# Weight loads issued from ScalarE's queue instead of SyncE's, with the list schedule's cost of such an issue changed

## The chip, the cores and the metric

The kernel runs on one core of a Trainium2 chip. The metric is device time in microseconds, the median of several executions. The engines are TensorE (PE; PEld is its weight load), VectorE (DVE), ScalarE (ACT), GpSimd (POOL) and SyncE (SP), which only issues DMA transfers. A q behind an engine's name (SPq, ACTq) is its instruction queue seen as an issuer of DMAs.

## What is computed

Three stages one after the other, on batch 4, sequence 576, model width 512 (8 heads of 64), in float32:

```
scores = scale * q @ k^T                      # 4 x 8 heads, 576 x 576
thresh = max(scores) - tau
scores = where(scores >= thresh, scores, -1e9)
attn   = softmax(scores) ;  x = attn @ v      # heads side by side: 4 x 576 x 512
h  = relu(x^T @ w_tok1) @ w_tok2              # mixes the tokens, 576 -> 256 -> 576
u  = x + h^T
x  = u + relu(u @ w_ch1) @ w_ch2              # 512 -> 1536 -> 512
h  = relu(x @ w_in)                           # 512 -> 1024
c  = 3-tap convolution of h along the sequence with conv_w
out = (h * sigmoid(c)) @ w_out                # 1024 -> 512
```

## The kernel before

**Arithmetic.** Most products run as three float16 passes over a high and a low half of each operand (`_h`, `_l`). Weights come from memory as float64 (two 32-bit words per element), are turned into float32 on the chip and split into halves. The scores of the first two batches are float32 matmuls.

**A piece of weights.** `load_hl` (L322) loads a piece of up to 128 x 512 elements (512 KB) into one of three buffers `st`. `wload` (L329) then turns it into float32 (`float32`, L355: ACT or POOL at L360/L362, ACT at L363, DVE at L364 and L366 into `wf`, of which there are two), makes the high half on ACT (L351) and the low half on POOL (L352). There are 47 such pieces, and the convolution's weights are one more small load through `load_hl`. A buffer `st` is free again when L363, L364 and L366 have read it, and only then may the load three pieces later start.

**Attention.** For each of 4 batches and 4 pairs of heads, `prep` (L441) loads `q`, `k` and `v` (`qt`, `kt`, `ld`); `scores` makes nine slots of 128 rows; `exps` takes the maximum on DVE (L548) and the exponential on ACT (L560), `mask` multiplies by the comparison on DVE (L567), `ph` and `rest` make two float16 halves (ACT L572, POOL L576), which a DMA transposes (L581; in the first batch inside `act_t`, later from `ph` to `pt`). `pv` multiplies by `v` (PE L591, L594), `norm` divides and splits into `xh` (ACT L619) and `xl` (POOL L620), `tok` does the token mixing.

**Dense part.** `dense(b)` holds both feed-forward layers of batch b (PE L758, L776, L809, L832). It runs beside the attention of batch b + 1. The first attention runs alone, with the first weight pieces beside it, up to about 106 us; the other pieces are turned beside `dense(0)`, up to about 280 us.

**Who orders the work.** All instructions are recorded first; then `Order.run` (L143) is a list scheduler: it keeps for each engine a time at which it is free, takes the earliest instruction by the program's order among those ready, adds a cost (`cost`, `send`), and fixes the order in which each engine issues. Each engine runs its own order strictly, so a waiting instruction holds all behind it. At most eight DMAs are under way in that order: eight semaphores (DMAHW0 to 7 below) serve all of them in turn. Before, SP issues every DMA except four small stores.

Of the kernel before, what the change touches and what calls it, by code (L numbers as in the profile page):

```python
# [11 lines left out]
I32 = mybir.dt.int32  # L12
# [8 lines left out]
class Order:  # L21
# [121 lines left out]
    def run(self):  # L143
        n = len(self.ins)
        left, ready, open_ = [len(b) for b in self.before], [0.0] * n, [False] * n
        later, now = {e: [] for e in self.LAG}, {e: [] for e in self.LAG}
        free, order = {e: 0.0 for e in self.LAG}, {e: [] for e in self.LAG}
        users, gone = {}, {}
        for u in self.uses:
            for t in u:  # L150
                users[t], gone[t] = users.get(t, 0) + 1, 0.0
        turn, slots, queue = {g: 0 for g in self.turns}, {g: [0.0] * self.bufs[g] for g in self.turns}, {g: [] for g in self.turns}
        end = start = queued = 0.0
        rows, tiled, lands = {}, False, []

        def offer(x):
            for t in self.first[x]:
                g = self.ring(t)
                if self.turns[g][turn[g]] != t or not slots[g]:
                    queue[g].append(x)  # L160
                    return
                ready[x] = max(ready[x], slots[g][0] + 40)
            open_[x] = True
            heapq.heappush(later[self.eng[x]], (ready[x], x))

        def again(g):
            held, queue[g] = queue[g], []
            for y in held:
                if not open_[y]:
                    offer(y)  # L170

        for x in range(n):
            if not left[x]:
                offer(x)
        for _ in range(n):
            t, e = min((free[e] if now[e] else max(free[e], later[e][0][0]), e) for e in free if now[e] or later[e])
            while later[e] and later[e][0][0] <= t:
                heapq.heappush(now[e], heapq.heappop(later[e])[1])
            x = heapq.heappop(now[e])
            if self.dma[x]:  # L180
                work, issue, least, land = self.send(x)
                if len(lands) >= 8:
                    t = max(t, lands[-8] + self.LAG["SP"])
                free[e] = t + 30 + issue
                if self.ins[x].opcode == "DmaTransposeAnt":
                    free[e] = max(free[e], queued)
                if e == "SP":
                    queued = max(queued, t + 700) + work
                    done = max(free[e] + least, queued + land)
                else:  # L190
                    done = max(free[e] + least, t + 700 + work + land)
                lands.append(done)
            elif e == "PE":
                work, (rt, ct), (r0, _) = self.cost(x), self.ins[x].tile_size, self.ins[x].tile_position
                wide = self.ins[x].ins[0].dtype == F32
                if rt < 128:
                    t = max(t, rows.get(r0, 0.0), start + 4, 0.0 if tiled else end + 95)
                    rows[r0], tiled = t + work, True
                    end, free[e] = max(end, t + work), t + 4
                else:  # L200
                    t = max(t, end + (95 if tiled else 0))
                    if ready[x] > end:
                        t = max(t, ready[x] + (250 if wide else 30))
                    rows, tiled, end, free[e] = {}, False, t + work, t + work
                start, done = t, t + work + 177
            else:
                work = self.cost(x)
                free[e], done = t + work - self.LAP[e], t + work + 12
            order[e].append(x)
            for z in self.first[x]:  # L210
                g = self.ring(z)
                turn[g] += 1
                heapq.heappop(slots[g])
                again(g)
            for z in self.uses[x]:
                users[z], gone[z] = users[z] - 1, max(gone[z], done)
                if not users[z]:
                    heapq.heappush(slots[self.ring(z)], gone[z])
                    again(self.ring(z))
            for z in self.after[x]:  # L220
                far = t + 1 if self.eng[z] == e == "PE" else done + self.LAG[self.eng[z]]
                ready[z] = max(ready[z], far)
                left[z] -= 1
                if not left[z]:
                    offer(z)
        for xs in order.values():
            for x, y in zip(xs, xs[1:]):
                self.tc.add_manual_dep(self.ins[y], self.ins[x].name, mybir.DependencyInfo(
                    mybir.DependencyClass.NoSync, mybir.DependencyReason.DATA), reason="order")
# [3 lines left out]
def kernel(ctx: ExitStack, tc: tile.TileContext, q, k, v, tau,  # L233
# [7 lines left out]
    nc = tc.nc  # L241
# [37 lines left out]
    V, A, G, T = nc.vector, nc.scalar, nc.gpsimd, nc.tensor  # L279
# [42 lines left out]
    def load_hl(src, o, n):  # L322

        st = stage.tile([P, 512, 2], I32, tag="st", name="st")
        nc.sync.dma_start(st[:, :n].rearrange("p n w -> p (n w)"), src.bitcast(I32)[:, 2 * o:2 * (o + n)])
        halves = st[:, :n].rearrange("p n w -> p (n w)").bitcast(U16).rearrange("p (n w) -> p n w", w=4)
        return halves[:, :, 1], st[:, :n, 1]

    def wload(src, dst, o, n, up, bank=None):  # L329

        hi, lo = [d[:, o:o + n] for d in dst]
        w = tmpp.tile([P, 512], F32, tag="wf", name="wf")[:, :n]
        if src.dtype == F32:
            nc.sync.dma_start(w, src[:, o:o + n])
            yield  # L340
            G.tensor_scalar(out=w, in0=w, scalar1=2.0 ** up, scalar2=1.0, op0=ALU.mult, op1=ALU.mult)
            whole = True
        else:
            lw, hw = load_hl(src, o, n)
            yield
            whole = up % 8 == 0
            f = ps[:, bank, :n] if bank is not None else w
            float32(w, f, lw, hw, up // 8, bank == CB)
        if not whole:
            G.tensor_scalar(out=w, in0=w, scalar1=2.0 ** up, scalar2=1.0, op0=ALU.mult, op1=ALU.mult)  # L350
        A.activation(out=hi, in_=w, func=AF.Copy)  # L351
        G.tensor_tensor(out=lo, in0=w, in1=hi, op=ALU.subtract)  # L352
        yield
# [51 lines left out]
    if conv_w.dtype == F32:  # L405
        nc.sync.dma_start(cw, conv_w)
    else:
        float32(cw, cw, *load_hl(conv_w, 0, 3 * NG), 0)
# [100 lines left out]
    free = [6]  # L509
# [363 lines left out]
    for b in range(B):  # L873
        att = attention(b + 1) if b + 1 < B else iter(())
        n = 0
# [66 lines left out]
```

## Time and profile before

| | before |
|---|---|
| median of 3 runs | 771.08 us (770.52 to 772.36) |
| the profiled execution | 773.05 us, span 771.2 us |
| PE busy | 721.5 us (94%) |
| DVE, ACT, POOL busy | 506.5, 459.0, 425.9 us |
| DMA share of the largest queue (SP's) | 58.2% |

The span runs from the first to the last instruction of the profiled execution; its own time has a little around it. In a timeline row stand start, duration, engine, line, operation, output<-inputs, and in brackets how long the engine stood idle before it and what ended that. The busy time of PE counts matmuls that overlap in the pipeline.

### The profile page before, as it was taken

Reading aid. Unit: us, or ns where it says so; the run is one execution under the profiler, and the core shown is the slowest. Engines: PE = TensorE matmul, PEld = TensorE weight load, DVE = VectorE, ACT = ScalarE, POOL = GpSimd, SP = SyncE. Lnnn points to the kernel's source line nnn. Section 1 sums busy time; section 2 is a strip of 40 time slices with the busy share of each in tenths; the row PEclk is TensorE's granted clock in tenths of the full one; section 3 lists DMA queues with packets and bytes.
Section 4 is the critical chain, followed back from the end, with each engine's and each line's share of the span. In section 5 each row is a group of like instructions: output and inputs, shape, how many; then the busy total and the mean of one; then the engine's idle time right before and its main releaser. Section 6 shows DMA issues by size and latency. Waiting matters only on the chain. (4 is left out here: it accounts for less than half of the span.)

```text
span 771.2 us, 18502 instructions
## 1 busy us (share of the span) xinstructions
PE 721.5 (94%) x7388; PEld 541.5 (70%) x7388; DVE 506.5 (66%) x913; ACT 459.0 (60%) x926; POOL 425.9 (55%) x463
## 2 busy tenths in 40 slices
PE   5779969999998789999999999999999999999998
PEld 3457757777776646788888766778888766878764
DVE  5968977887779971676867962676876951323470
ACT  6967857786758852576557753675656841211371
POOL 5967778887877990367464850367564830000040
PEclk9999989999999999999999999999999999999999
DMA  9999988999898602568876402577853400000001
GB/s 288 210 217 187 200 193 208 230 230 229 199 238 199 147 27 93 111 153 169 155 142 144 80 23 88 131 136 158 155 123 64 79 29 35 1 1 2 1 1 62
DMA packets 196199, 99.02 MB, mean 128 GB/s; under 512 B 174224, under 2 KB 177808, under 8 KB 196112
## 3 DMA queue, kind: packets, MB, share of 16 engines
q1 hardware_dynamic: 195792, 97.57, 58.2%
q8 instruction: 58, 0.95, 0.5%
q10 hardware_dynamic: 320, 0.26, 0.1%
q14 instruction: 29, 0.24, 0.1%
HBM read 43.54 MB, written 4.72 MB: 63 GB/s over the span
## 5 line engine op out<-in xcount | busy, mean ns | idle before, releaser
L576 POOL TENSOR_TENSOR ph<-e,ph 128x576 f16<-128x576 f32 x108 | 142.5, 1319 | 110.4 <-ACT ph L572 99.3
L776 PE MATMUL ps<-act_t,wc_h 128*128 128x256 f16 (+1 forms) x768 | 149.8, 286 | 0.0
L567 DVE SCALAR_TENSOR_TENSOR e<-ps,thr,e 128x576 f32<-128x576 f32 x108 | 87.9, 814 | 53.6 <-ACT e L560 40.8
L548 DVE TENSOR_REDUCE nm<-ps 128x1 f32<-128x576 f32 x144 | 108.0, 750 | 19.6 <-PE ps L536 10.5
L799 POOL TENSOR_TENSOR act_t<-ct,act_t 128x576 f16<-128x576 f32 x32 | 47.2, 1474 | 128.4 <-ACT act_t L798 127.0
L758 PE MATMUL ps<-u_h,wc_h 128*128 128x320 f16 (+1 forms) x384 | 109.4, 286 | 0.3 <-DVE act_t L733 0.3
L776 PE MATMUL ps<-act_t,wc_l 128*128 128x256 f16 (+1 forms) x384 | 109.7, 286 | 0.0
L758 PE MATMUL ps<-u_h,wc_l 128*128 128x320 f16 (+1 forms) x384 | 109.5, 286 | 0.0
L758 PE MATMUL ps<-u_l,wc_h 128*128 128x320 f16 (+1 forms) x384 | 109.1, 286 | 0.0
L758 PEld LDWEIGHTS <-wc_h 128*128 128x128 f16 x768 | 75.1, 98 | 21.5 <-issue 2.1
L776 PEld LDWEIGHTS <-wc_h 128*128 128x128 f16 x768 | 75.1, 98 | 21.0 <-issue 1.6
L809 PE MATMUL ps<-u_h,wi_h 128*128 128x256 f16 (+1 forms) x256 | 73.2, 286 | 7.1 <-ACT h L785 4.5
L832 PE MATMUL ps<-wo_h,act_t 128*128 128x512 f16 x256 | 76.2, 379 | 0.9 <-POOL act_t L799 0.9
L794 DVE SCALAR_TENSOR_TENSOR ct<-h,cw,ct 128x576 f32<-128x576 f32 x64 | 70.6, 1106 | 8.2 <-ACT ct L792 7.7
L572 ACT ACTIVATE ph<-e 128x576 f16<-128x576 f32 x108 | 73.1, 677 | 1.0 <-DVE e L567 0.8
L733 DVE SCALAR_TENSOR_TENSOR act_t<-ps,act_t 128x256 f16<-128x256 f32 x96 | 43.6, 456 | 45.2 <-ACT act_t L732 44.8
L809 PE MATMUL ps<-u_h,wi_l 128*128 128x256 f16 (+1 forms) x256 | 73.1, 286 | 0.0
L809 PE MATMUL ps<-u_l,wi_h 128*128 128x256 f16 (+1 forms) x256 | 73.1, 286 | 0.0
L591 PE MATMUL ps<-vh,pt 128*128 128x65 f16 (+1 forms) x1080 | 68.3, 194 | 1.0 <-DVE x L614 0.8
L732 ACT ACTIVATE act_t<-ps 128x256 f16<-128x256 f32 x96 | 39.0, 408 | 46.1 <-PE ps L758 45.4
L832 PEld LDWEIGHTS <-act_t 128*128 128x128 f16 x384 | 36.5, 98 | 42.7 <-POOL act_t L799 1.5
L591 PEld LDWEIGHTS <-pt 128*128 128x128 f16 (+1 forms) x1080 | 60.8, 101 | 8.0 <-issue 4.7
(120 smaller groups left out, 1675.0 us busy)
## 6 DMA issues: line engine op xcount, KB each, us to landing
st<-in_moe_w_ch_dram SPq DMA_DIRECT2D x24, 512.0 KB, 4.8
ld<-in_v_dram SPq DMA_DIRECT2D x32, 288.0 KB, 4.1
kt<-ks SPq DMA_DIRECT2D x32, 144.0 KB, 2.8
st<-in_moe_w_in_dram SPq DMA_DIRECT2D x8, 512.0 KB, 4.7
st<-in_moe_w_out_dram SPq DMA_DIRECT2D x8, 512.0 KB, 4.2
out_dram<-ot SPq DMA_DIRECT2D x16, 256.0 KB, 2.0
qt<-in_q_dram SPq DMA_DIRECT2D x8, 288.0 KB, 5.2
kt<-in_k_dram SPq DMA_DIRECT2D x16, 144.0 KB, 4.2
```

Source lines behind the costliest of these rows:

```text
L548: V.tensor_reduce(out=nm, in_=c["s3"], axis=AX.XY, op=ALU.max, negate=True)
L567: V.scalar_tensor_tensor(out=e3, in0=c["s3"], scalar=c["thr"], in1=e3, op0=ALU.is_ge, op1=ALU.mult)
L572: A.activation(out=c["ph"][:, 0:S], in_=c["e"], func=AF.Copy)
L576: G.tensor_tensor(out=c["ph"][:, S:], in0=c["e"], in1=c["ph"][:, 0:S], op=ALU.subtract)
L591: T.matmul(dst[o:o + m], pt[:, j, o:o + m], vh[:, hh, j, 0:D + 1], start=(j == 0), stop=(j == NSL - 1))
L733: V.scalar_tensor_tensor(out=r_t(f, 1)[:, sl], in0=t, scalar=0.0, in1=r_t(f, 0)[:, sl], op0=ALU.max, op1=ALU.subtract)
L758: T.matmul(t, wc1[wx][:, f, c], u[c][ux][:, sl], start=(c == 0 and i == 0), stop=(c == NC - 1 and i == 2))
L776: T.matmul(t, wc2[wx][:, c, f], r_t(f, rx)[:, sl], start=(by_dve(c) and f == 0 and i == 0), stop=(f == NF - 1 and i == 2))
L794: V.scalar_tensor_tensor(out=ct, in0=ht[:, kk:kk + S], scalar=cw[:, kk, f:f + 1], in1=ct, op0=ALU.mult, op1=ALU.add)
L799: G.tensor_tensor(out=g_t(f, 1), in0=ct, in1=g_t(f, 0), op=ALU.subtract)
L809: T.matmul(t, wi[wx][:, f, c], u[c][ux][:, s0:s0 + n], start=(c == 0 and i == 0), stop=(c == NC - 1 and i == 2))
L832: T.matmul(t, g_t(f, gx)[:, j * P:(j + 1) * P], wo[wx][:, f], **lim)
```

## The change

`load_hl` issues its load from ACT's queue. In the list schedule an issue that is not SP's is placed at the time when its inputs are ready, but not before `began`, the start of the last ACT instruction placed, and ACT is free again after that issue or after its own work, whichever is later.

```diff
-        end = start = queued = 0.0
+        end = start = queued = began = 0.0
...
                 work, issue, least, land = self.send(x)
                 if len(lands) >= 8:
                     t = max(t, lands[-8] + self.LAG["SP"])
-                free[e] = t + 30 + issue
+                if e != "SP":
+                    t = max(ready[x], began)
+                free[e] = max(free[e], t + 30 + issue)
...
             else:
                 work = self.cost(x)
+                began = t if e == "Activation" else began
                 free[e], done = t + work - self.LAP[e], t + work + 12
...
         st = stage.tile([P, 512, 2], I32, tag="st", name="st")
-        nc.sync.dma_start(st[:, :n].rearrange("p n w -> p (n w)"), src.bitcast(I32)[:, 2 * o:2 * (o + n)])
+        A.dma_start(st[:, :n].rearrange("p n w -> p (n w)"), src.bitcast(I32)[:, 2 * o:2 * (o + n)])
```

Three lines are added in `run`, so a line number of the kernel below it is three higher in the changed kernel. The new costs give a new order on all engines up to about the end of `dense(0)`; the number of instructions is the same.

SP's order at the start, before (`qt_157`, `kt_0_158`, `kt_1_159` are the first pair of heads, `qt_160`, `kt_0_161`, `kt_1_162` the second; what a row waits for stands in brackets):

```order
L483 DMA ld<-in_v_dram 128x576 x2
L447 DMA qt_160<-in_q_dram 128x576
L452 DMA kt_0_161<-in_k_dram 64x576 [waits DMAHW0_49]
L452 DMA kt_1_162<-in_k_dram 64x576 [waits DMAHW1_49]
L483 DMA ld<-in_v_dram 128x576 [waits DMAHW2_49]
L483 DMA ld<-in_v_dram 128x576 [waits DMAHW3_49]
L325 DMA st<-in_moe_w_tok_dram 128x1024 [waits DMAHW4_49]
```

and in the changed kernel:

```order
L486 DMA ld<-in_v_dram 128x576 [waits DMAHW1_49]
L450 DMA qt_160<-in_q_dram 128x576 [waits DMAHW2_49]
L455 DMA kt_0_161<-in_k_dram 64x576 [waits DMAHW3_49]
L455 DMA kt_1_162<-in_k_dram 64x576 [waits DMAHW4_49]
L486 DMA ld<-in_v_dram 128x576 [waits DMAHW5_49]
L486 DMA ld<-in_v_dram 128x576 [waits DMAHW6_49]
```

The weight loads that stood behind these rows on SP now stand at the head of ACT's order and hold semaphores 0, 3 and 5 of the first round, so that `qt_160` now waits for the landing of `qt_157` (semaphore 2), `kt_0_161` for that of the first weight load and the next `ld` for that of the second.

SP's order at the end of the first attention, before (the load of `kt_1_162` in two halves for the next batch):

```order
L447 DMA qt_160<-in_q_dram 128x576 [waits PE_49]
L455 DMA kt_1_162<-in_k_dram 64x2x288 [waits DMAHW3_49]
L581 DMA_TRANSPOSE act_t<-act_t 128x9x128 [waits DMAHW4_49,Pool_49]
L581 DMA_TRANSPOSE act_t<-act_t 128x9x128 [waits DMAHW5_49,DMAHW6_49,PE_49,Pool_49]
L581 DMA_TRANSPOSE act_t<-act_t 128x9x128 [waits DMAHW7_49,PE_49,Pool_49]
L581 DMA_TRANSPOSE act_t<-act_t 128x9x128 [waits DMAHW1_49,PE_49,Pool_49]
L325 DMA st<-in_moe_w_ch_dram 128x1024 [waits DMAHW0_49,DVE_49]
L455 DMA kt_1_162<-in_k_dram 64x2x288
```

and in the changed kernel:

```order
L450 DMA qt_160<-in_q_dram 128x576 [waits PE_49]
L458 DMA kt_1_162<-in_k_dram 64x2x288 [waits DMAHW2_49]
L584 DMA_TRANSPOSE act_t<-act_t 128x9x128 [waits DMAHW3_49,Activation_49,Pool_49]
L584 DMA_TRANSPOSE act_t<-act_t 128x9x128 [waits DMAHW4_49,Pool_49]
L584 DMA_TRANSPOSE act_t<-act_t 128x9x128 [waits DMAHW5_49,DMAHW6_49,PE_49,Pool_49]
L584 DMA_TRANSPOSE act_t<-act_t 128x9x128 [waits DMAHW0_49,PE_49,Pool_49]
L458 DMA kt_1_162<-in_k_dram 64x2x288
L584 DMA_TRANSPOSE act_t<-act_t 128x9x128 [waits DMAHW1_49,DMAHW3_49,PE_49,Pool_49]
```

Between the four transposes and the second half the weight load is gone. Ahead of `qt_160`, back to the loads of `kt_0_161`, there are now two transposes where there were three and a weight load, and the last transpose of the stage now stands behind the second half.

ACT's order at the same place, before:

```order
L363 ACTIVATE ps<-st 128x512 [waits DMAHW0_49,DVE_49]
L351 ACTIVATE wc_h<-wf 128x512 [waits Pool_49]
L461 ACTIVATE kt_1_162<-kt_1_162,qsc 128x576 [waits DMAHW3_49,DMAHW1_49]
L619 ACTIVATE xh<-x_1292 128x4x64 [waits DVE_49]
L560 ACTIVATE e<-ps,nm 128x576 [waits PE_49]
```

and in the changed kernel:

```order
L464 ACTIVATE kt_1_162<-kt_1_162,qsc 128x576 [waits DMAHW2_49,DMAHW0_49]
L563 ACTIVATE e<-ps,nm 128x576 [waits DVE_49]
L328 DMA st<-in_moe_w_ch_dram 128x1024 [waits DVE_49,Activation_49]
L366 ACTIVATE ps<-st 128x512
L575 ACTIVATE ph<-e 128x576
L354 ACTIVATE wc_h<-wf 128x512 [waits Pool_49]
L622 ACTIVATE xh<-x_1292 128x4x64 [waits DVE_49]
```

Between `kt_1_162` and the last `xh` of this attention there now stand an exponential, a weight load and three more activations. Of the 48 loads on ACT, 13 stand ahead of this `kt_1_162` row, four of them ahead of the first `qt_157` row; 12 of the 48 name DVE among what they wait for.

## Rows read from the trace of the kernel before

**Rows 1.** The page, part 1: busy time, share of the span, instructions
```profile
PE 721.5 (94%) x7388; PEld 541.5 (70%) x7388; DVE 506.5 (66%) x913; ACT 459.0 (60%) x926; POOL 425.9 (55%) x463
```

**Rows 2.** Busy by stretch: PE, PEld, DVE, ACT, POOL, clock, DMA share, GB/s
```profile
20.00:106.00 86.00, 67.12 (x860) 49.86 (x861) 71.78 (x161) 65.84 (x121) 68.02 (x71) 0.98 1.08 205
...
120.00:240.00 120.00, 117.69 (x1245) 88.49 (x1245) 97.42 (x191) 87.48 (x168) 97.61 (x107) 1.00 0.97 225
```

**Rows 3.** Sums of waits of PE: us in total, times, longest
```profile
PE ps L591 <- DMA act_t<-act_t: 11.0, 8, 2.9
```

**Rows 4.** Timeline of PE, 31 to 108 us: five of its waits
```profile
31.51 0.22 PE L591 MATMUL ps<-vh,act_t 128*64 128x65 f16 x1 [1.11 <-DMA act_t<-act_t]
...
38.78 0.20 PE L591 MATMUL ps<-vh,act_t 128*128 128x65 f16 x1 [1.43 <-DMA act_t<-act_t]
...
49.82 0.20 PE L591 MATMUL ps<-vh,act_t 128*128 128x65 f16 x1 [2.89 <-DMA act_t<-act_t]
...
103.98 0.20 PE L591 MATMUL ps<-vh,act_t 128*128 128x65 f16 x1 [2.47 <-DMA act_t<-act_t]
107.15 0.69 PE L631 MATMUL ps<-xh,wt_h 128*128 128x128 f16 x5 [1.89 <-ACT xh L619]
```

**Rows 5.** Timeline of SP's queue, 28 to 102 us: issues
```profile
28.09 0.53 SPq L325 DMA_DIRECT2D st<-in_moe_w_tok_dram  x1
...
33.22 0.52 SPq L325 DMA_DIRECT2D st<-in_moe_w_tok_dram  x1
...
40.88 1.01 SPq L325 DMA_DIRECT2D st<-in_moe_w_ch_dram  x2
41.98 7.71 SPq L581 DMA_TRANSPOSE act_t<-act_t  x3
...
93.64 6.63 SPq L581 DMA_TRANSPOSE act_t<-act_t  x4
100.36 0.54 SPq L325 DMA_DIRECT2D st<-in_moe_w_ch_dram  x1
100.96 0.64 SPq L455 DMA_DIRECT2D kt<-in_k_dram  x1
```

**Rows 6.** Landing of the transpose at 41.98 us, then of 72 between 300 and 620 us
```profile
DMA to landing us min/median/max: 7.8/7.8/7.8
...
DMA to landing us min/median/max: 3.2/3.3/5.5
```

**Rows 7.** Timeline of ACT, 99 to 109 us
```profile
106.02 0.77 ACT L461 ACTIVATE kt<-kt,qsc 128x576 f32<-128x576 f32 x1 [2.87 <-DMA kt<-in_k_dram]
```

**Rows 8.** Busy by stretch, 106.5 to 113 us; the seventh column is the granted clock
```profile
106.50:113.00 6.50, 5.85 (x47) 4.54 (x47) 3.57 (x8) 4.47 (x9) 5.08 (x6) 0.50 0.79 183
```

**Rows 9.** Timelines of ACT and SP, the first 10 us
```profile
0.73 1.28 ACT L284 ACT_TABLE_LOAD   x1 [0.73 <-PEq L926]
...
5.45 0.77 ACT L461 ACTIVATE qt<-qt,qsc 128x576 f32<-128x576 f32 x1 [1.52 <-DMA qt<-in_q_dram]
...
9.81 0.78 ACT L461 ACTIVATE qt<-qt,qsc 128x576 f32<-128x576 f32 x1 [0.18 <-DMA qt<-in_q_dram]
...
4.47 0.43 SPq L447 DMA_DIRECT2D qt<-in_q_dram  x1
...
6.10 1.06 SPq L483 DMA_DIRECT2D ld<-in_v_dram  x2
```

**Rows 10.** Timeline of ACT, 306 to 307 us: a store issued by ACT
```profile
306.19 0.38 ACT L653 ACTIVATE u_h<-ps 128x256 f16<-128x256 f32 x1
306.20 0.56 ACTq L823 DMA_DIRECT2D out_dram<-ot  x1
306.87 0.77 ACT L438 ACTIVATE qs<-ld,qsc 128x576 f16<-128x576 f32 x1 [0.29 <-ACT u_h L653]
```

**Rows 11.** Sums of waits of SP's queue; DMA issues of the first 40 us
```profile
SPq L325 <- DVE wf L366: 16.9, 11, 3.2
...
st<-in_moe_w_tok_dram SPq DMA_DIRECT2D x2, 512.0 KB, 6.7
```

## The prediction

> **What bounds the kernel now.** I read the page first: TensorE is busy 721.5 us of the span [rows 1], so a change that moves no arithmetic can only win where PE stands still. The table by stretches says where that is [rows 2]: from 120 to 240 us PE is busy nearly all the time (117.69 of 120.00 us), but in the first attention, from 20 to 106 us, it is busy 67.12 of 86.00 us, while ACT is busy 65.84. So I looked at what PE waits for there. In the sums of waits the largest is the PV matmul at L591 waiting for the DMA that transposes `act_t`: 11.0 us in 8 waits [rows 3], which the timeline places between 31 and 104 us [rows 4].
>
> Then I asked why those transposes are late, in the timeline of SP's queue [rows 5]. SP issues every load of the kernel but a few in one row. At 40.88 us it issues two weight loads of 512 KB, and at 41.98 us a transpose: that one lands after 7.8 us, where the 72 transposes from 300 to 620 us, with no weight load near, land after a median of 3.3 us [rows 6]. PE waits for it at 49.82 us. The waits at 31.51 and 38.78 us have the same picture: loads at 28.09 and 33.22 us stand directly ahead of the transposes.
>
> The fourth thing to see is the hole at the end of this stage. At 100.36 us SP issues a weight load and only then, at 100.96 us, the second half of `kt_1_162` [rows 5]. ACT, which runs in order, stands 2.87 us for it [rows 7], with `xh` behind it; PE waits 1.89 us for `xh` at 107.15 us [rows 4]. PE had waited 2.47 us just before (103.98 us), and from 106.5 to 113 us the granted clock is 0.50, the lower level of 1.2 GHz [rows 8].
>
> **The change part by part.** 48 weight loads leave SP and stand on ACT, 13 of them ahead of the end of the first attention. Arithmetic, tiles and bytes stay as they are.
>
> *Loads out of SP's line, minus 2.7 us.* Three waits of PE have a weight load directly ahead of the transpose in SP's queue: 1.11 + 1.43 + 2.89 = 5.43 us [rows 4]. The transposes now start without these in their line, but the same bytes still go over the same 16 engines at the same time, so I take half. Nothing at all is one end, 5.4 us the other. That two lines share the engines instead of standing behind each other is not shown by this trace, since ACT's line carries only four stores of 64 KB in it. The Trainium skill, DMA: Bandwidth & Descriptors, section "Queues, rings and completion order", says that each engine takes packets from the rows with work in turn, and that SP and ACT own a row each; by it a transpose would share instead of queue, and the half would stand.
>
> *The hole, minus 1.9 us.* In the order shown above, the second `kt_1_162` load no longer has the weight load ahead of it, and one transpose that stood ahead of it now stands behind. The load's issue and the gap to the next is 100.96 - 100.36 = 0.60 us, and the four transposes ahead take SP 6.63 us, 1.66 each [rows 5], so the data come about 2.3 us earlier, which covers the 1.89 us that PE waits. Ends: 0 (ACT has one more `e` and a load of its own between `kt` and `xh` now) and 1.9. If the gap closes so far that the clock does not fall, half of the 6.5 us at 0.50 is won on top, 3.2 us; I count none of it, because the wait of 2.47 us before it stays, and keep it for the range.
>
> *The start, plus 1.0 us.* Eight semaphores (DMAHW0 to 7) serve all loads in turn, and a load waits for the one eight places ahead. Three weight loads that stood late in the line now stand early on ACT. So `qt_160`, which SP issued at 4.47 us, now waits for the landing of `qt_157`, which ACT saw at 5.45 us [rows 9]: 1.0 us later, and ACT's conversion of it (9.81 us, ended by the landing) stands ahead of the first exponentials. One end is 0, as ACT converts weights meanwhile that it converted later before. The other: the `ld` load that SP issued at 6.10 us [rows 9] waits for the second weight load; issued behind ACT's table load, which ends at 2.0 us, and behind the first weight load's issue, so at about 2.9 us, and with 6.7 us to land [rows 11], that is 9.6 us, 3.5 us later.
>
> *The issue on ACT, plus 1.3 us.* The trace has this operation: ACT's own store issue starts at 306.20 us, beside the activation of 306.19, takes 0.56 us, and the next activation finds ACT idle for 0.29 us [rows 10]. Nine of the issues lie between 20 and 106 us: 9 x 0.29 = 2.6 us, of which I put half on the path, since ACT and PE are both busy three quarters of that stage [rows 2]. Ends: 0 (behind a 0.63 us activation the issue is fully covered) and 9 x 0.56 = 5.0 us. The other 35 lie beside PE that has work without gaps; if that cover fails they cost 35 x 0.29 = 10 us.
>
> SP is also free of 48 issues of about 0.5 us. That is priced at nothing beyond the terms above: SP mostly waits for POOL to finish the tile that it is to transpose. What is late next after the transposes is POOL itself.
>
> **Sum:** -2.7 - 1.9 + 1.0 + 1.3 = -2.3 us. The profiled execution took 773.05 us, of which 771.2 is span; it would be 770.75. The median of the three runs is 1.97 us lower than the profiled one, so I set the forecast against it: 771.08 - 2.3 = 768.8 us. I count a difference under 0.2% (1.54 us) as none.
>
> **The rivals.** (1) *The same engines, so nothing is won.* The bytes and their instants stay, and the profile shows the DMA engines busy all through the stage (share 1.08 from 20 to 106 us) [rows 2]. Then the first term is 0, the hole gains the 0.60 us of SP's time alone, and start and issues cost 2.3 us: 771.08 - 0.6 + 1.0 + 1.3 = 772.8 us with both costs in full, 770.5 us if both are hidden. For it: the engines' share. Against it: the 7.8 us of a transpose right behind loads against 3.3 us. The same page of the Trainium skill, section "Issuing engines are not separate DMA queues", says that initiating DMAs on several engines only saves the sequencer's time; that is this rival, and it speaks against the change.
>
> (2) *A waiting issue holds ACT: slower.* ACT runs in order, and a load may only go out once DVE has read the buffer of three loads ago. On SP such waits took 16.9 us in 11 times, up to 3.2 us [rows 11], and cost little since only transposes stood behind. On ACT the exponentials and the weight conversions stand behind. In the changed order 12 of the 48 issues name DVE among their waits. If they wait as long as on SP and half of it reaches PE, it is +8.4 us: 771.08 - 2.3 + 8.4 = 777.2 us. It decides from 2.3 us on the path, a seventh of those 16.9 us. For it: the activations are on the longest chain of this stage. Against it: most issues stand behind the conversion to `wc_h` of the same piece, which waits for that very DVE instruction anyway, and ACT reaches such a place later than SP did.
>
> (3) *The issue does not run alongside.* The order counts on ACT's issue overlapping its work; one row shows that. If it took its full 0.56 us of ACT, 9 x 0.56 = 5.0 us in the first stage: 771.08 - 2.3 + 3.7 = 772.5 us.
>
> **How the numbers follow.** Forecast 0.47, rival 1 0.26, rival 2 0.18, rival 3 0.09. The forecast's own range is 764 to 770. Faster by over 0.2% comes from the forecast: 0.47. No change takes most of rival 1 and some of rival 3: 0.25. Slower takes rival 2 and what is left of 1 and 3: 0.28. All good ends together (5.4, 1.9 and 3.2) would give 760.6 us, all bad ones (3.5 and 5.0) 779.6; the range of 763.5 to 776.0 leaves out the far ends of both and most of rival 2.
>
> **What would show it.** Right: in the profile after, PE's waits for the transposes of `act_t` fall from 11.0 us to 8 or less, no transpose between 20 and 106 us lands after more than 6 us, ACT waits for `kt` under 1.5 us at the end of the first attention, and the hole there is shorter. The first exponential starts at 11 to 12 us. ACT's issues of about 0.5 us have idle of under 0.3 us behind them. Wrong: landings of 7 us stay (rival 1), ACT's issues show waits for DVE over 1 us with PE idle behind them (rival 2), or ACT stands 0.5 us at each issue (rival 3). If PE gains in the first stage and loses it again between 240 and 285 us, where it is not full either, the forecast is wrong in a way that no term here holds.

## The result, and the profile after

The changed kernel takes 783.22 us (median of 20 runs, 777.53 to 793.58); the kernel before, run beside it, 771.88 us. The ratio is 1.0133, 95% interval 1.0108 to 1.0157: slower by 1.3%, outside the range of the prediction. The ratios, here and below, leave out runs of more than 1.5% above the fastest of their kernel, so that a ratio is not quite the quotient of the medians beside it. The profiled execution took 779.91 us with a span of 778.1 us, 6.9 us more than that of before. From L210 on, the changed kernel's lines have a number higher by 3.

The page's first part and the table by stretches answer to [rows 1] and [rows 2]; the columns are those shown there.

```profile
PE 725.6 (93%) x7388; PEld 542.4 (70%) x7388; DVE 505.9 (65%) x913; ACT 459.9 (59%) x926; POOL 425.6 (55%) x463
```

```profile
20.00:106.00 86.00, 67.85 (x847) 49.41 (x846) 72.50 (x157) 65.94 (x121) 66.28 (x69) 0.98 1.05 200
120.00:240.00 120.00, 113.03 (x1163) 83.71 (x1161) 92.44 (x185) 83.84 (x161) 95.65 (x106) 1.00 0.98 213
```

No engine has more instructions; PE's busy time is 4.1 us more for the same 7388. The second row shows a change: from 120 to 240 us PE was busy 117.69 us and is now busy 113.03 us, where the prediction counted on PE having work without gaps. The first row hides one: PE is as busy as before in this stretch, but the stage ends later, as the part on how the loss adds up tells.

The sums of waits of PE from 20 to 110 us (us in total, times, longest) answer to [rows 3], and the timeline of PE to [rows 4].

```profile
PE ps L594 <- DMA act_t<-act_t: 14.5, 9, 2.9
```

```profile
53.77 0.20 PE L594 MATMUL ps<-vh,act_t 128*128 128x65 f16 x1 [2.84 <-DMA act_t<-act_t]
...
96.25 0.20 PE L594 MATMUL ps<-vh,act_t 128*128 128x65 f16 x1 [2.06 <-DMA act_t<-act_t]
108.38 0.20 PE L594 MATMUL ps<-vh,act_t 128*128 128x65 f16 x1 [2.88 <-DMA act_t<-act_t]
...
138.51 0.30 PE L761 MATMUL ps<-u_h,wc_h 128*128 128x320 f16 x1 [1.56 <-DVE act_t L736]
141.43 0.27 PE L761 MATMUL ps<-u_h,wc_h 128*128 128x256 f16 x1 [1.12 <-DVE act_t L736]
```

The waits for the transposes of `act_t`, which were to fall from 11.0 us to 8 or less, rose to 14.5 us. To see why, read when each transfer was issued and when it landed. First ACT, 44 to 47 us, then SP's queue, 43 to 60 us:

```profile
44.16 0.74 ACT L563 ACTIVATE act_t<-ps,nm 128x576 f32<-128x576 f32 x1
44.54 0.34 ACTq L328 DMA_DIRECT2D st<-in_moe_w_ch_dram  x1
44.78 0.45 ACT L354 ACTIVATE wt_h<-wf 128x288 f16<-128x288 f32 x1
44.92 0.56 ACTq L328 DMA_DIRECT2D st<-in_moe_w_ch_dram  x1
45.12 0.42 ACT L622 ACTIVATE xh<-x 128x256 f16<-128x256 f32 x1
45.52 0.45 ACTq L328 DMA_DIRECT2D st<-in_moe_w_ch_dram  x1
```

```profile
41.80 8.92 SPq L584 DMA_TRANSPOSE act_t<-act_t  x3
```

The second of these three transposes was issued at 44.21 us, 0.3 us ahead of ACT's first load. Its landing is the first row below (the DMA view of 44.2 to 44.3 us). The second row holds shortest, median and longest landing of all transposes of `act_t` from 20 to 110 us; in the kernel before the longest was the 7.8 us of [rows 6].

```profile
act_t<-act_t SPq DMA_TRANSPOSE x1, 9.5
```

```profile
DMA to landing us min/median/max: 3.2/4.1/11.0
```

So a transpose that was issued *ahead* of the load landed after 9.5 us. From a second queue a load seems to slow what is already on its way, and not only what stands behind it; the experiments test that. The loads suffer too: the one of 45.52 us took 10.2 us. Counted over the two traces from 20 to 290 us, 6 of 70 transposes landed later than 6 us before, and 15 of 70 after; from 290 to 640 us, where no weights are loaded, it is none of 72 in both.

The two waits near 140 us come from late transfers by another way. The DMA view of 125.8 to 126.8 us, and ACT's timeline:

```profile
st<-in_moe_w_ch_dram ACTq DMA_DIRECT2D x1, 512.0 KB, 8.4
pt<-ph SPq DMA_TRANSPOSE x1, 9.5
```

```profile
133.21 0.38 ACT L735 ACTIVATE act_t<-ps 128x256 f16<-128x256 f32 x1 [0.76 <-PE ps L761]
135.36 0.34 ACTq L328 DMA_DIRECT2D st<-in_moe_w_ch_dram  x1
135.75 0.74 ACT L563 ACTIVATE e<-ps,nm 128x576 f32<-128x576 f32 x1 [2.15 <-POOL wf L353]
...
139.87 0.78 ACT L464 ACTIVATE kt<-kt,qsc 128x576 f32<-128x576 f32 x1 [1.41 <-DMA kt<-in_k_dram]
```

The transpose issued at 125.81 us landed 9.5 us later, at 135.3 us. The load at 135.36 us shares a completion semaphore with it (the eight semaphores that serve all transfers in turn), so it had to wait for that landing, and ACT stood from 133.59 to 135.36 us with an exponential, and behind that the channel stage's relu outputs `act_t`, in its row. The view names POOL as releaser, whose instruction was not over; the program's wait and the landing's time show that it was the transfer. PE's wait of 1.56 us follows. Ahead of the one of 1.12 us ACT stood 1.41 us for a load of `kt` on SP's queue, which was issued at 133.04 us, beside all these, and landed after 6.7 us.

### The profile page after: what moved, and what is told of

It is laid out like the page before. It is cut to its first block, busy times and chain, and to the rows that moved or that the text cites. A ratio compares the mean times of both kernels' runs of the same rounds, so it can differ in the third digit from the quotient of the medians.

```text
span 778.1 us, 18476 instructions
## 1 busy us (share of the span) xinstructions
PE 725.6 (93%) x7388; PEld 542.4 (70%) x7388; DVE 505.9 (65%) x913; ACT 459.9 (59%) x926; POOL 425.6 (55%) x463
## 5 line engine op out<-in xcount | busy, mean ns | idle before, releaser
L761 PE MATMUL ps<-u_l,wc_h 128*128 128x256 f16 (+1 forms) x384 | 109.2, 286 | 0.0
L797 DVE SCALAR_TENSOR_TENSOR ct<-h,cw,ct 128x576 f32<-128x576 f32 x64 | 69.5, 1088 | 10.2 <-ACT ct L795 9.7
```

What stands on the lines that cost most here:

```text
L761: T.matmul(t, wc1[wx][:, f, c], u[c][ux][:, sl], start=(c == 0 and i == 0), stop=(c == NC - 1 and i == 2))
L797: V.scalar_tensor_tensor(out=ct, in0=ht[:, kk:kk + S], scalar=cw[:, kk, f:f + 1], in1=ct, op0=ALU.mult, op1=ALU.add)
```

## The experiments

Three theories stood against each other: **Q**, two queues in flight at once make the transposes late; **P**, the new plan of the order costs; **S**, the late start costs.

### The order kept, only the queue changed

```diff
-        self.eng = [str(i.engine).split(".")[-1] for i in self.ins]
+        self.moved = {x for x, i in enumerate(self.ins) if i.opcode == "DMACopy" and self.area(i.outs[0])[0].startswith("st")}; self.eng = ["SP" if x in self.moved else str(i.engine).split(".")[-1] for x, i in enumerate(self.ins)]
...
-            order[e].append(x)
+            order["Activation" if x in self.moved else e].append(x)
...
-        for xs in order.values():
+        for xs in (sorted(o, key=begin.get) for o in order.values()):
...
-        nc.sync.dma_start(st[:, :n].rearrange("p n w -> p (n w)"), src.bitcast(I32)[:, 2 * o:2 * (o + n)])
+        A.dma_start(st[:, :n].rearrange("p n w -> p (n w)"), src.bitcast(I32)[:, 2 * o:2 * (o + n)])
```

> The loads are issued by ACT, but every engine keeps the order of the kernel before: the loads are planned as if they were SP's, and each is put into ACT's row at its planned instant. PE, DVE and POOL have row for row the order of before. Theory Q (two queues in flight at once make the transposes late): the loss stays, 776 to 783 us, and of the transposes from 20 to 290 us ten or more land later than 6 us (6 of 70 in the kernel before, 15 of 70 in the changed one). Theory P (the new plan is what costs, above all the three loads within 1 us at 44.6 us): 771 to 773 us and at most 7 such transposes. Theory S (the start costs: PE's first matmul at 8.84 us where it was 6.32): 771 to 773 us too, since the loads of the start stand as late as before and the first matmul comes at about 6.3 us.

Measured: 788.35 us against 772.29 us, ratio 1.0165 (1.0111 to 1.0219). 15 of 71 transposes from 20 to 290 us landed later than 6 us, the longest after 11.9 us. The end of the first attention, in PE's timeline and in the DMA view of 99.6 to 101.7 us:

```profile
105.17 0.23 PE L591 MATMUL ps<-vh,act_t 128*128 128x65 f16 x1 [4.41 <-DMA act_t<-act_t]
...
109.90 0.24 PE L591 MATMUL ps<-vh,act_t 128*128 128x65 f16 x1 [3.80 <-DMA act_t<-act_t]
```

```profile
st<-in_moe_w_ch_dram ACTq DMA_DIRECT2D x1, 512.0 KB, 8.0
act_t<-act_t SPq DMA_TRANSPOSE x1, 10.2
```

With PE, DVE and POOL in the very order of before, the move to ACT alone costs as much as the whole change. P is out as the main cause. As PE's rows are the same in both traces, they can be laid side by side: this kernel is 0.2 us ahead at the matmul of 97.28 us of before, 5.9 us behind at that of 103.98 us, and 14.2 us behind at the end.

### Which loads cost

```diff
-        A.dma_start(st[:, :n].rearrange("p n w -> p (n w)"), src.bitcast(I32)[:, 2 * o:2 * (o + n)])
+        (A if len(loads) <= 13 else nc.sync).dma_start(st[:, :n].rearrange("p n w -> p (n w)"), src.bitcast(I32)[:, 2 * o:2 * (o + n)])
```

The two other kernels have `nc.sync if len(loads) <= 13 else A` and `nc.sync if len(loads) <= 4 else A` there.

> Only the first 13 loads (those up to the end of the first attention) are issued by ACT, the other 35 by SP; the plan's rule is that of the changed kernel. Theory Q: the part of the loss that stands at the end of the first attention in the changed kernel stays (its last PV matmul there starts 4.4 us later than before), the part behind it does not: 774 to 778 us. Theory S: 773 to 775 us, all of it already there at the first matmul. Theory P in the sense that any other plan costs: 776 to 783 us.

> The first 13 loads are issued by SP, the other 35 by ACT. Theory Q: the first attention is that of before, and from 110 to 290 us the loss is what the changed kernel loses there, 2.6 to 7 us: 774 to 778 us, with at least 5 of the 35 transposes from 110 to 290 us later than 6 us (3 before, 7 changed). Theory S: 771 to 773 us. If 35 issues on ACT beside a gapless PE cost nothing, as the prediction had it: 771 to 773 us.

> Only the first four loads (the convolution's weights and the three of the first token matrix) go back to SP, the other 44 stay on ACT. Theory S: the first matmul is back at about 6.3 us, and the time falls by at least half of the loss, to 772 to 777 us. Theory Q: the first matmul is back at 6.3 us, but the changed kernel had made up for its late start by 22 us (its first PV matmul at 22.21 us against 23.43 us), so the time stays at 778 to 784 us.

| loads on ACT | time, us | ratio (95%) | longest transpose, 20 to 110 us | 110 to 290 us |
|---|---|---|---|---|
| none (before) | 772.29 | 1 | 7.8 | 6.6 |
| first 13 | 775.34 | 1.0041 (1.0013 to 1.0068) | 9.7 | 6.5 |
| last 35 | 777.12 | 1.0057 (1.0036 to 1.0078) | 7.1 | 9.6 |
| all but 4 | 786.83 | 1.0143 (1.0100 to 1.0187) | 9.9 | 9.4 |

The long landings, of over 9 us, stand where the loads of the second queue are, and only there. Both parts cost, and the later one, beside a PE that should have had work enough, costs as well. One expectation of Q failed: with the first 13 loads on ACT, the last PV matmul of the first attention starts only 0.2 us later than before, not 4.4, and the profile loses its time after 240 us, where these loads are long over. So the 0.4% of this part is not shown to come from late transposes; the new order of the later part can have cost it. Where a late transpose hits PE depends on the order around it.

S is out: with four loads back on SP, PE starts as early as ever (6.32 us before), and the time is no better.

```profile
5.95 1.30 PE L530 MATMUL ps<-kt,qt 128*128 128x288 f32 x2 [5.95 <-ACT qt L464]
```

The plan's new rule alone, with all loads on SP, changes nothing:

> The plan's new rule for issues by ACT, with all loads still on SP; the rule then bears on the four stores of the outputs alone. All theories: within 0.2% of the kernel before, 770 to 774 us. If it is off by more, the rule has an effect that none of the other runs has taken apart.

Measured: 771.75 us against 770.63 us, ratio 1.0005 (0.9984 to 1.0025).

### The same load on either queue, in a stage without any

```diff
+    def extra(e):
+        st = stage.tile([P, 512, 2], I32, tag="st", name="st")
+        G.tensor_scalar(out=st[:, 0, 0:1].bitcast(F32), in0=e[:, 0:1], scalar1=1.0, scalar2=1.0, op0=ALU.mult, op1=ALU.mult)
+        nc.sync.dma_start(st.rearrange("p n w -> p (n w)"), w_ch1.bitcast(I32)[:, 0:1024])
...
     def rest(i):
         c = chk[i]
+        if i >= 2 * PER and i % 6 == 0:
+            extra(c["e"])
         G.tensor_tensor(out=c["ph"][:, S:], in0=c["e"], in1=c["ph"][:, 0:S], op=ALU.subtract)
+        if i >= 2 * PER and i % 6 == 3:
+            extra(c["e"])
```

The second kernel has `A.dma_start` in `extra`, put in its planned place as in the first experiment.

> The kernel before with 24 more loads of 512 KB, read from the first channel matrix into the staging tile and used by nobody, in the stage of 290 to 640 us that has no weight load: one with every third softmax tile, right behind or right ahead of the transpose, issued by SP. Theory Q: with one queue a load holds up the transposes behind it and no others; few of the 72 transposes land later than 6 us (at most 8; none without the loads, median 3.32 us) and the longest stays under 8 us, the 7.8 us of before. If loads and transposes disturb each other whichever queue they stand in: as many and as long as with the loads on ACT.

> The same 24 loads at the same places of the plan, issued by ACT; PE, DVE and POOL have row for row the order of the run beside it. Theory Q: 12 or more of the 72 transposes land later than 6 us, the longest later than 9 us, and the loads themselves take longer to land than on SP. If the queue makes no difference: as on SP. The time is no measure here, since PE has work without gaps in this stage in both.

Measured on SP: 779.48 us (one run), 2 of the 72 transposes later than 6 us, the longest 6.3 us. On ACT: 795.72 us (one run), 7 later than 6 us, two of them after 13.5 and 13.2 us. The kernel before, run beside both, took 770.63 us. Q holds in kind, not in number: I had expected 12 or more. Nor is the time without meaning, as I had written: PE is not gapless enough to hide 13 us. PE's rows are the same in these two kernels, and side by side they show what each of the two latest transposes costs. First ACT and PE of the kernel with the loads on ACT, then its row by stretches:

```profile
385.58 0.68 ACT L572 ACTIVATE ph<-e 128x576 f16<-128x576 f32 x1 [7.38 <-DMA pt<-ph]
389.28 0.22 PE L601 MATMUL ps<-vh,pt 128*128 128x65 f16 x1 [6.31 <-DVE x L624]
```

```profile
387.70:394.50 6.80, 5.22 (x47) 3.83 (x47) 5.61 (x12) 3.85 (x9) 4.18 (x7) 0.50 0.81 191
```

Up to 377.93 us of the kernel on SP the two are level to within 1.7 us (there to 0.04 us). Then ACT stands 7.4 us until the late transpose has read its `ph`, PE 6.3 us behind it, and the clock falls to 0.50: the matmul of 385.18 us starts at 393.56 us, 8.4 us later. At the second place the distance goes from 7.7 us (555.13 and 562.78 us) to 16.1 us (562.38 and 578.51 us), and at the end it is 16.3 us. Though each is one run, the difference of the two times, 16.2 us, thus arises at these two places, and the lower clock is part of it.

Then the same with all 24 behind a transpose in the plan, with each only after the landing of its own tile's transpose, and on POOL's queue:

```diff
-        if i >= 2 * PER and i % 6 == 0:
-            extra(c["e"])
...
-        if i >= 2 * PER and i % 6 == 3:
+        if i >= 2 * PER and i % 3 == 0:
             extra(c["e"])
```

```diff
         nc.sync.dma_start_transpose(out=c["pt"], in_=c["ph"])
+        if i >= 2 * PER and i % 3 == 0:
+            extra(c["pt"][:, 0, 0:2].bitcast(F32))
```

```diff
-        A.dma_start(st.rearrange("p n w -> p (n w)"), w_ch1.bitcast(I32)[:, 0:1024])
+        G.dma_start(st.rearrange("p n w -> p (n w)"), w_ch1.bitcast(I32)[:, 0:1024])
```

> The 24 extra loads on ACT again, now all of them right behind a transpose of the same tile (in the run before, 12 stood behind and 12 ahead; the two transposes of over 13 us there, at 372 and 557 us, were followed by a load within 0.7 us, and no load that stood ahead had such a landing). If a load on ACT that is issued while a transpose has just begun is what makes both slow: about twice as many, 3 to 6 transposes with 9 us or more, and the time is above 800 us. If it was chance, or the copies from qs to qt that stood near them: one to three such transposes, around 795 us.

> The 24 extra loads on ACT, each only once the transpose of its tile has landed (its staging tile is first written from the transposed tile). If what costs is a load that is issued while a transpose is under way: no transpose lands later than 9 us, at most 3 later than 6 us, and the time is near the 779.5 us of the extra loads on SP. If two queues cost in themselves: as with all of them behind a transpose.

> The 24 extra loads at the same places as in the run with all of them right behind a transpose, issued by POOL's queue, which the profile calls software_dynamic, where ACT's and SP's are hardware_dynamic. With all weight loads on POOL only 6 transposes from 20 to 290 us landed later than 6 us, the longest after 7.3 us. If it is ACT's queue beside SP's that slows the transposes: none over 9 us here, and under 785 us. If any second queue does: as on ACT.

Measured: 794.80, 782.94 and 792.21 us (one run each); the longest transposes landed after 13.8, 11.4 and 12.3 us. The first of them did not separate what it was to separate: in its trace 7 of the 24 loads came within 1 us behind a transpose, as many as in the run with half of them planned there. In both runs 2 of these 7 transposes were late by far, so "a transpose has just begun" is not the whole condition. Waiting for a tile's own transpose did not keep the transposes early, as the next one is soon issued: 12 landed later than 6 us. Yet this run is the shortest of the four with a second queue, so what a late transpose costs depends on what waits for it. And POOL's queue, which I had held harmless, makes one such pair of a late transpose and a late load as well (the last rows of this section). With one pair, most of that run's 20.6 us over the kernel before (771.66 us) likely has another cause, as in the run with all weight loads on POOL below. What a pair is shows best at one place of the work, on either queue: first the table by stretches, from the transpose's issue to the last landing, then the DMA view of the two. On ACT (the run with all loads behind a transpose):

```profile
371.50:384.40 12.90, 10.76 (x122) 8.36 (x120) 5.78 (x11) 3.86 (x9) 1.97 (x4) 1.00 1.15 144
```

```profile
st<-in_moe_w_ch_dram ACTq DMA_DIRECT2D x1, 512.0 KB, 11.9
pt<-ph SPq DMA_TRANSPOSE x1, 12.8
```

The same place with the load on SP (the first of the two kernels above):

```profile
371.90:378.10 6.20, 5.37 (x78) 4.43 (x77) 2.86 (x6) 3.34 (x8) 1.57 (x2) 1.00 0.99 260
```

```profile
st<-in_moe_w_ch_dram SPq DMA_DIRECT2D x1, 512.0 KB, 4.8
pt<-ph SPq DMA_TRANSPOSE x1, 4.7
```

And with the load on POOL, 373.2 to 373.7 us:

```profile
st<-in_moe_w_ch_dram POOLq DMA_DIRECT2D x1, 512.0 KB, 11.9
ld<-in_k_dram SPq DMA_DIRECT2D x1, 288.0 KB, 4.7
pt<-ph SPq DMA_TRANSPOSE x1, 12.3
```

In the last two columns of the stretches the DMA engines are busy all the time (share 1.15 and 0.99), but move 144 GB/s when transpose and load come from two queues, and 260 GB/s when they come from one. Side by side they don't just share the engines: a packet takes longer on average (2523 packets at a share of 1.15 over 12.9 us make 94 ns each, 1967 at 0.99 over 6.2 us make 50 ns; both stretches hold other transfers too), and both transfers end together, 12 to 13 us later, where one behind the other they end within some 6 us.

### When a pair forms

Eleven profiles have loads on ACT's queue. In them 129 transposes are followed by such a load within 2 us. In 54 every earlier transfer had landed when the load was issued, and none of these transposes took 8.5 us or more. In 75 an earlier transfer was still on its way, and 22 did. Twelve more transposes took as long without a load so close behind: each was issued while such a pair, or its loads, were still on their way. Counted the same way in the four profiles with all loads on SP, 72 transposes have a load within 2 us behind them, 48 with an earlier transfer on its way, and the longest of them took 7.5 us. I tried to make the pair on purpose, with five loads and then two:

```diff
-        if i >= 2 * PER and i % 3 == 0:
+        if i in (80, 89, 98, 116, 125):
             extra(c["e"])
```

The others have `(78, 87, 96, 114, 123)` and `(90, 126)`; the last pair runs once on ACT and once on SP.

> Five extra loads on ACT, each planned right behind the transpose that follows the two loads of q and k (288 KB each) on SP. In all runs so far, every transpose of 8.5 us or more had a load of the other queue issued within 2 us of it while an earlier transfer was still on its way (or stood right behind such a transpose), so that transpose and load had to start together. If that is the condition: at least 3 of these 5 transposes land later than 8.5 us, and the run is 5 us or more longer than the one with the loads aside. If place doesn't matter and one load in ten does it by chance: none or one.

> The same five loads on ACT, each planned right behind a transpose that stands between other transposes, two ahead of the loads of q and k, with no other load near. If the condition is right: no transpose from 290 to 640 us lands later than 8.5 us and the time is 771 to 775 us. If a transpose and a load of the other queue in flight together are enough by themselves: as many as in the other of the two.

> Only two of the extra loads, on ACT: those of tiles 90 and 126, at whose place both runs with 24 loads on ACT had their two worst landings (13.5 and 13.2 us, 12.8 and 13.8 us). There SP has just issued the loads of q and k (288 KB each, still on their way) and a transpose, and ACT's load follows the transpose within 0.7 us. If that is the condition, and not the number of loads: both transposes land later than 8.5 us again and the time is 5 us or more above that of the same two loads on SP. If it came from 24 loads together, or by chance: none or one, and no difference over 2 us. The run with five loads aimed at such places does not answer it, as its loads came 1.3 to 3 us ahead of the transpose instead of behind it.

> The same two loads at the same places of the plan, issued by SP; PE, DVE and POOL have row for row the same order. All theories: no transpose from 290 to 640 us later than 7 us, and 770 to 775 us.

Measured: 770.49 and 770.08 us (one run each) with five loads, and longest landings of 6.3 and 6.2 us; 770.74 us (ratio 1.0000, 0.9983 to 1.0017) and 769.90 us (0.9988, 0.9975 to 1.0001) with two, longest 5.5 and 5.9 us. Both attempts missed: the five loads came 1.3 to 3 us ahead of the aimed transpose, and the two came 1.3 to 1.4 us behind it instead of 0.7, when the loads of q and k had landed or did so within 0.4 us. The control stands: in the second run with five loads, a load 0.9 us behind a transpose, with nothing else on its way, delays both, but not past 6.2 us (DMA view of 361.4 to 362.4 us).

```profile
st<-in_moe_w_ch_dram ACTq DMA_DIRECT2D x1, 512.0 KB, 5.3
pt<-ph SPq DMA_TRANSPOSE x1, 6.2
```

So a load on a second queue can be free: these five cost no time in the one run (772.5 us before, one run beside it). That an earlier transfer must be on its way, so that transpose and load start together, rests on the count; it wasn't made to happen at will.

### All weight loads on POOL

> The order of the kernel before, with each load issued by POOL at its planned instant. If it is ACT's queue or ACT's time that costs: 771 to 775 us, as POOL is busy 425 us of 771 only. If any second queue beside SP's makes the transposes late (theory Q): 10 or more of the 70 transposes from 20 to 290 us land later than 6 us and the time is 776 us or more, with POOL's own issues on top, which no run has shown yet.

The edit is the first experiment's with "Pool" in the place of "Activation" and `G.dma_start`. Measured: 796.01 us against 770.63 us, ratio 1.0341 (1.0271 to 1.0412), with 6 of 69 transposes later than 6 us, the longest after 7.3 us. Q had expected 10 or more. No pair formed in this profile, so the loss has another cause. The likely one is POOL, which stands ahead of each transpose and here issues itself and waits itself. The first row is from the view of L325 (shortest, median and longest issue in ns), the second from POOL's timeline.

```profile
L325 POOL DMA_DIRECT2D st<-in_moe_w_ch_dram x24: 535/604/613, 41.8 to 198.9; - x24
```

```profile
111.93 0.61 POOL L325 DMA_DIRECT2D st<-in_moe_w_ch_dram  x1 [5.26 <-DVE x L611]
```

How its 25 us divide between these two was not taken apart.

## Why the prediction was wrong

**Loads out of SP's line: this is the step that failed.** I took half of three waits off, -2.7 us, with 0 as the worst end. PE's waits for these transposes rose by 3.5 us (11.0 to 14.5). The error is in "the transposes now start without these in their line, but the same bytes still go over the same 16 engines at the same time": I took the engines' work as a fixed sum that two lines divide. It grows when a transpose and a load run side by side (12.9 us against 6.2 us for the same pair). No row of before showed two busy queues, so the term's worst end should have been a loss; I set it at 0 without a reason. For the half I had leaned on the Trainium skill, DMA: Bandwidth & Descriptors, section "Queues, rings and completion order", by which engines take packets of the rows in turn. That fits what is seen so far as the two of the pair land within 0.2 us of each other (384.3 and 384.1 us), but it says nothing on what taking turns costs, and here that decides.

One of the three waits was also misread. PE's wait at 31.51 us ended with the landing of this transpose, which stands ahead of the load of 28.09 us in SP's queue [rows 5]:

```profile
26.50 1.49 SPq L581 DMA_TRANSPOSE act_t<-act_t  x1
```

So that load cannot have held it, and the load ahead of it, of 23.78 us, landed 0.4 us after its issue: 1.11 of the 5.43 us had no good reason to stand in the sum.

**The hole: the wait named is gone, the hole is a little shorter.** ACT waited 2.87 us for `kt_1_162` [rows 7]; now it waits for nothing there:

```profile
103.98 0.60 ACT L622 ACTIVATE xh<-x 128x256 f16<-128x256 f32 x2
104.64 0.78 ACT L464 ACTIVATE kt<-kt,qsc 128x576 f32<-128x576 f32 x1
```

But the transpose that moved behind `kt` is issued at 101.90 us, 0.7 us after ACT's load of 101.21 us, and lands after 6.4 us; PE waits 2.88 us for it at 108.38 us, in place of the 1.89 us for `xh` [rows 4]. With 0.99 us at 109.97 us the waits add up to 3.9 us, where 2.47 and 1.89 us made 4.4, and the clock is at 0.50 for 3.4 us from 110.1 us, where it was for 6.8 us. So the term had the right sign and, in waits, a quarter of its size. I had named what is late next, and not costed it.

**The start: within its bounds, and of no account.** The first exponential starts at 13.01 us, 2.5 us later (I had said 11 to 12), since ACT issued two loads of 512 KB at 1.25 and 1.66 us, already during its table load, and PE's first matmul waited for `kt` until 8.84 us: the loads of `kt` landed after 7.0 us, before after 3.6 and 4.1 us. But PE's first PV matmul came at 22.21 us, before at 23.43 us, and putting those loads back gained nothing. A delay of the first instructions is not a delay of the stage.

**The issue on ACT: too high.** An issue takes 0.33 us beside ACT's own work, as at 101.21 us, where nothing stands still:

```profile
100.88 0.73 ACT L563 ACTIVATE e<-ps,nm 128x576 f32<-128x576 f32 x1
101.21 0.33 ACTq L328 DMA_DIRECT2D st<-in_moe_w_ch_dram  x1
101.59 0.66 ACT L366 ACTIVATE ps<-st 128x512 int32<-128x512 uint16 x1
```

In 34 of the 48 cases the next activation found ACT idle for less than 0.05 us. That disposes of rival 3. Rival 2, a waiting issue holds ACT, was the nearest in time (777.2 us) but not in kind: ACT was held for 1.8 us once, by the landing of a late transpose and not by DVE's reading of the buffer. Rival 1 was right that nothing is won from the same engines (no run with loads on ACT was faster beyond the noise), and wrong that nothing is lost. The Trainium skill, DMA: Bandwidth & Descriptors, section "Issuing engines are not separate DMA queues", names saved sequencer time as the only gain, which agrees. The loss behind the first attention is one that no term held; the prediction's last sentence looked for such a thing between 240 and 285 us only.

**How it adds up.** Against before, the profiled execution stands 4.4 us behind at the last PV matmul of the first attention, 5.8 us in the middle of the first channel stage (at 148.5 us of the changed kernel), 6.6 us at 234 us and 7.0 us at the end. The largest step ahead of the hole is the wait of 2.06 us at 96.25 us, for a transpose that landed after 7.3 us. The clock falls behind it, where it stayed at 1.00 before:

```profile
96.40:99.80 3.40, 3.40 (x26) 2.14 (x24) 1.83 (x5) 1.97 (x4) 1.89 (x2) 0.51 1.12 205
```

A matmul ahead of this place starts 1.7 us later than before (92.14 and 93.84 us), one behind it 5.5 us later (94.36 and 99.83 us). The median stands 4.4 us further behind than this profile does (11.3 against 6.9 us). The runs go with the granted clock, though not strictly: the four at 0.991 and above took 777.5 to 780.8 us, the four at 0.981 and below 787.4 to 793.6 us, and one at 0.987 took 791.5 us. That late transposes open gaps behind which the clock falls is shown at 96.4 us here and at 387.7 us above. That the longer executions have more such places is likely, but only one of these executions has a trace here.

## What to carry to other kernels

Before a transfer is moved to another engine's queue, look for what is in flight beside it: one queue is an order, and an order protects the transfer that PE waits for. A second queue can double the time of both transfers (12.9 us against 6.2 us here), though the engines show a share of 1 or more in either case; read GB/s beside the share. To tell a queue's effect from a new plan's, keep every other engine's order row for row and move the issue alone; the two traces can then be laid side by side, and the time is lost where the distance between equal rows grows.

## What was not expected of the hardware

A transpose of 3.2 us and a load of 512 KB of about 4 us, from two queues, ended together after 12.8 us, with the DMA engines at a share of 1.15 and 144 GB/s, and elsewhere after up to 13.8 us; with all loads in one queue no transpose of this kernel took over 7.8 us. It is rare (22 of 129 transposes with a load close behind), was seen only with an earlier transfer on its way, and appears with POOL's queue too. An issue on ACT took 0.33 us where the store of [rows 10] took 0.56 us, and in 34 of 48 cases left no idle time behind it.
